# The last mode's product with weights stationary and spectrum moving, straight into Y^T, in a one-core spectral kernel on Trainium2

## The chip, the cores and the metric

The kernel runs on one core of one Trainium2 chip. The metric is device time in microseconds (us) of one execution. The kernel before took 433.02 us, the median of three runs (432.55 to 433.25).

## The reference, cut to what matters

A linear attention (8 batches, 8 heads, 576 rows, head size 64) gives x of 8 x 576 x 512. Then comes a spectral mix: a real Fourier transform over the 576 rows, and for each of the 64 lowest modes a complex product with that mode's own 512 x 512 weights.

```python
Yr = np.einsum('bmd,mde->bme', Xr, w_r) - np.einsum('bmd,mde->bme', Xi, w_i)
Yi = np.einsum('bmd,mde->bme', Xr, w_i) + np.einsum('bmd,mde->bme', Xi, w_r)
...
y = np.fft.irfft(Y, n=S, axis=1)
u = x + y
return (u + np.maximum(u @ w_ch, 0.0)).astype(np.float32)
```

The weights are 2 x 64 matrices of 1 MB in float32. They are each used once, for 8 batches. So the kernel is a stream of weights with little arithmetic per byte. The output stage needs all modes, because the inverse transform sums over them.

## The kernel before

Each mode's product has the spectrum as the stationary operand (32 columns of `xt_c`, of which 16 are wanted: real and imaginary parts of 8 batches) and the weights moving. The four 128-row chunks `dc` of the contraction run side by side in four column strips of the array: in the trace of before, the first four of the last eight products start within 10 ns of each other, at 394.05 us, where whole-array products of the same width (zl) start 109 to 120 ns apart. Their partial sums lie in four groups of 32 partitions. A second set of small "pick" products adds the groups and transposes the result.

```python
def mode_product(kk, ps, stage, yt_ps):
    wr, wi = w_get(kk)
    st = stage.tile([128, D], F16, tag="ystage", bufs=2, name=f"ys{kk}")
    n_part = 2 if kk == NM - 1 else 1          # the last mode: two halves of the columns
    pw = D // n_part
    P = [ps.tile([128, D], F32, tag="P", bufs=2, ...)[:, 0:pw] for i in range(n_part)]
    for t, w in ((1, wr), (0, wi)):
        for i in range(n_part):
            for dc in range(NDC):
                mm = nc.tensor.matmul(
                    P[i][dc * 32 : dc * 32 + 32, :], xt_cols(dc, t, kk),
                    w[:, dc, i * pw : i * pw + pw],
                    start=(t == 1), stop=(t == 0), tile_position=(0, dc * 32))
        if t == 1 and kk >= NM - 4:
            keep_warm(6)                       # products nobody needs, for PE's clock
    if NM - 4 <= kk < NM - 1:
        keep_warm(3)
    for i in range(n_part):                    # casts, VectorE or ScalarE
        dst = st[:, i * pw : i * pw + pw]
        if (kk + i) % 2 == 0: nc.vector.tensor_copy(out=dst, in_=P[i])
        else:                 nc.scalar.copy(out=dst, in_=P[i])
    for ec in range(NDC):                      # sum of four groups, transposed
        mm = nc.tensor.matmul(yt_ps[:, ec, kk % 8, :], st[:, ec * 128 : ec * 128 + 128], pick_sb)
    ...
```

A copy then moves `yt_ps` into `YT` (Y^T: columns of the model on partitions). After the last mode the output stage begins. It forms `zl` from the last eight modes of `YT` and the channel weights, stages it in `last`, and adds the inverse transform into accumulators (`acc`), which are rectified, added and stored.

```python
def keep_warm(n):
    for _ in range(n):
        pin(nc.tensor.matmul(last_ps[0], id16, wch16[:, 0, :]))
...
for h in range(2):                             # zl: first product of the output stage
    for ec in range(NDC):
        nc.tensor.matmul(last_ps[h][:, 0:hw], rows[ec], wch16[:, ec, cols], ...)
```

Weights are loaded by GpSimd-issued DMAs that cast to bfloat16, eight buffers deep, one DMA for each matrix.

Of the kernel before, what the change touches and what calls it, by code (L numbers as in the profile page):

```python
# [10 lines left out]
F32 = mybir.dt.float32  # L11
# [36 lines left out]
def kernel(  # L48
# [10 lines left out]
    nc = tc.nc  # L59

    B, H, S, Dh = q.shape
    D = H * Dh
    NM = moe_w_r.shape[0]
    NHP = H // 2
    NDC = D // 128
    NJJ = 4
    XDC = 3 * B * NM
    XTW = NDC * XDC + 2 * B * NM
    NL = 8
# [23 lines left out]
    xt_c = xpool.tile([128, XTW], BF16, name="xt_c")  # L93
# [3 lines left out]
    def xt_cols(dc: int, t: int, kk: int):  # L97

        c0 = dc * XDC + t * B * NM + kk
        return xt_c[:, c0 : c0 + 31 * NM + 1 : NM]  # L100
# [9 lines left out]
    def w_load(kk: int, half: int, pool, tag: str, bufs: int):  # L110
        name, src = (("wr", moe_w_r), ("wi", moe_w_i))[half]
        w = pool.tile([128, NDC, D], BF16, tag=tag, bufs=bufs, name=f"{name}{kk}")
        tc.keep_in_program_order(
            nc.gpsimd.dma_start(out=w, in_=src[kk].rearrange("(p dc) e -> p dc e", dc=NDC))  # L114
        )
        return w

    w_in: dict[int, list] = {}
# [9 lines left out]
    pin = tc.keep_in_program_order  # L128
# [5 lines left out]
    def w_next():  # L134
        kk, half = pending.pop(0)
        pool, tag, bufs = (wpool, "w", W_KEEP) if kk < n_keep else (wpre, "wp", W_PRE)
        w_in.setdefault(kk, []).append(w_load(kk, half, pool, tag, bufs))
# [187 lines left out]
    def w_get(kk: int):  # L325
        if kk not in w_in:
            w_in[kk] = [w_load(kk, half, wpool, "w", W_KEEP) for half in range(2)]
        return w_in.pop(kk)

    def keep_warm(n: int):  # L330

        for _ in range(n):
            pin(nc.tensor.matmul(last_ps[0], id16, wch16[:, 0, :]))

    def mode_product(kk: int, ps, stage, yt_ps):

        wr, wi = w_get(kk)
        st = stage.tile([128, D], F16, tag="ystage", bufs=2, name=f"ys{kk}")

        n_part = 2 if kk == NM - 1 else 1  # L340
        pw = D // n_part
        P = [
            ps.tile([128, D], F32, tag="P", bufs=2, name=f"P{kk}_{i}")[:, 0:pw] for i in range(n_part)
# [7 lines that stand above are left out]
                        start=(t == 1), stop=(t == 0), tile_position=(0, dc * 32),  # L351
                    )
                    if kk >= NM - 4:
                        pin(mm)
            if t == 1 and kk >= NM - 4:
                keep_warm(6)
# [4 lines that stand above are left out]
            if (kk + i) % 2 == 0:  # L361
                nc.vector.tensor_copy(out=dst, in_=P[i])  # L362
            else:
                nc.scalar.copy(out=dst, in_=P[i])  # L364
        for ec in range(NDC):
            mm = nc.tensor.matmul(  # L366
                yt_ps[:, ec, kk % 8, :], st[:, ec * 128 : ec * 128 + 128], pick_sb
            )
            if kk >= NM - 4:
                pin(mm)  # L370
        if NM - 4 <= kk < NM - 1:
            keep_warm(3)

    while pending:
        w_next()
    tc.keep_in_program_order(
# [6 lines left out]
    psW = tc.alloc_tile_pool(name="psW", bufs=1, space=PSUM, side="left")  # L383
# [9 lines left out]
    YT = ystage.tile([128, NDC, NM, 2 * B], F16, name="YT")  # L393
    yt_ps = None

    def mode(kk: int):
        nonlocal yt_ps
        if kk % 8 == 0:
            yt_ps = psW.tile([128, NDC, 8, 2 * B], F32, tag="yt", bufs=1, name=f"yt{kk // 8}")
        mode_product(kk, psW, ystage, yt_ps)  # L400
        if kk == NM - 2:
            nc.vector.tensor_copy(out=YT[:, :, NE : NM - 1, :], in_=yt_ps[:, :, 0 : NL - 1, :])
        elif kk == NM - 1:
            nc.vector.tensor_copy(out=YT[:, :, NM - 1, :], in_=yt_ps[:, :, NL - 1, :])  # L404
        elif kk % 8 == 7:
            nc.vector.tensor_copy(out=YT[:, :, kk - 7 : kk + 1, :], in_=yt_ps)

    for kk in range(n_early):
        mode(kk)
# [192 lines left out]
    for kk in range(n_early, NM):  # L602
        mode(kk)
        want = min(len(tiles), (kk - n_early + 1) * len(tiles) // n_spread)
        while done < want:
            channel_product(tiles[done])
            done += 1
        if kk >= NE - 1:
            while rows_done < min(B, 2 * (kk - NE + 2)):
                form_rows(rows_done)  # L610
                rows_done += 1
        if kk == NM - 5:
            psB.release()
            acc_pools.append(
                tc.alloc_tile_pool(name="psT0", bufs=1, space=PSUM, side="right", reuse_waits="tile")
            )
            for n in range(N_PRE):
                channels(n)
                for i, t in enumerate(pairs[n]):
                    add_inverse(n, i, t, 1, EARLY)  # L620
            last_ps.append(psW.tile([128, D], F32, tag="zl", bufs=1, name="zl0"))
# [6 lines left out]
    for h in range(2):  # L628
        cols = slice(h * hw, h * hw + hw)
        for ec in range(NDC):  # L630
# [3 lines left out]
                    start=(ec == 0), stop=(ec == NDC - 1),  # L634
# [62 lines left out]
```

## Time and profile before

| What | Value | View |
|---|---|---|
| Time | 433.02 us median | timed runs |
| Last weights landed | 394.01 us after the span's start | chain |
| First zl product | 395.65 us | timeline |
| Last PE work | about 422 us | chain |
| End of the span | 430.9 us | page |

In the views PE is TensorE's matmuls, PEld its weight loads, DVE VectorE, ACT ScalarE, POOL GpSimd and SP SyncE; L348 is line 348 of the kernel. The span is the time from the first instruction to the last. The page's second part cuts it into 40 slices. A digit is the busy share in tenths; PEclk is the granted TensorE clock, in tenths of full speed.

```profile
PE   0357867787018777677776767667787678997992
...
PEclk9996676666559766657658577566555866999997
DMA  8999999999999999999999999999999999993797
GB/s 148 207 208 209 209 209 209 211 213 215 222 211 213 216 212 213 213 213 213 213 214 214 213 213 213 214 214 214 214 214 213 213 213 213 214 213 77 292 330 281
```

DMA is saturated from the second slice to the 36th, at almost one rate. No engine is over the whole of that stretch. The stream of weights sets when the output stage can start. In slices 37 to 39 PE is at 7, 9 and 9 tenths, at full clock.

The chain that ended last, that is the last instruction followed back through what released each step (start, length, what), shows the joint between the two stages:

```profile
377.26 16.75 DMA wi<-in_moe_w_i_dram
...
394.05 0.39 PE P L348 x4
...
394.52 0.38 ACT ys L364
...
394.95 0.40 PE yt L366 x4
...
395.37 0.23 DVE YT L404
...
395.65 1.06 PE zl L632 x8
```

The timeline of the same stretch (start, length, engine, line, operation, output<-inputs, shapes, and in brackets the idle time before it and what ended it):

```profile
394.05 0.48 PE L348 MATMUL P<-wi,xt_c 128*32 128x256 bf16 x8 [0.54 <-DMA wi<-in_moe_w_i_dram]
...
394.52 0.37 ACT L364 CAST ys<-P 128x256 f16<-128x256 f32 x1 [8.32 <-PE P L348]
394.64 0.42 DVE L362 CAST ys<-P 128x256 f16<-128x256 f32 x1 [3.27 <-PE P L348]
...
394.95 0.39 PE L366 MATMUL yt<-pick_sb,ys 128*128 128x16 f16 x4 [0.42 <-ACT ys L364]
395.37 0.22 DVE L404 CAST YT<-yt 128x64 f16<-128x64 f32 x1 [0.30 <-PE yt L366]
```

Four engine steps follow each other after the landing, each waiting for the one before: products, casts, pick products, copy. From landing to zl they take 395.65 - 394.01 = 1.64 us. This text calls that the tail.

### The profile page before, as it was taken

How to read it: one execution, taken by the hardware profiler on the slowest of the kernel's cores; microseconds unless marked ns; L12 is line 12 of the kernel's file. 1: busy time of each engine (PE TensorE's matmuls, PEld its weight loads, DVE VectorE, ACT ScalarE, POOL GpSimd, SP SyncE). 2: the span in 40 equal slices, each digit the busy share in tenths (PEclk: the TensorE clock that was granted, in tenths of full speed). 3: DMA queues.
4: the chain of work that ended last, by engine and by line, in shares of the span. 5: the costliest groups of instructions: out<-in, count | busy, mean ns of one | idle time of the engine just before them, and what ended most of it. 6: DMA issues, size and time to landing. Idle time of an engine off the chain costs nothing. (4 is left out here: it accounts for less than half of the span.)

```text
span 430.9 us, 6215 instructions
## 1 busy us (share of the span) xinstructions
PE 297.7 (69%) x2542; PEld 154.3 (36%) x2542; DVE 176.9 (41%) x334; ACT 147.3 (34%) x228; POOL 92.3 (21%) x166
## 2 busy tenths in 40 slices
PE   0357867787018777677776767667787678997992
PEld 0346656564004233222322223222233226833440
DVE  0699998854004242322322222322223212202793
ACT  3587666631003222222223213222222221302781
POOL 4233232112102222211222112222212221200100
PEclk9996676666559766657658577566555866999997
DMA  8999999999999999999999999999999999993797
GB/s 148 207 208 209 209 209 209 211 213 215 222 211 213 216 212 213 213 213 213 213 214 214 213 213 213 214 214 214 214 214 213 213 213 213 214 213 77 292 330 281
DMA packets 35563, 92.38 MB, mean 214 GB/s; under 512 B 3152, under 2 KB 16336, under 8 KB 35536
## 3 DMA queue, kind: packets, MB, share of 16 engines
q0 software_dynamic: 32016, 82.52, 98.4%
q1 hardware_dynamic: 3520, 9.47, 5.9%
q8 instruction: 20, 0.33, 0.3%
q14 instruction: 7, 0.06, 0.0%
HBM read 164.07 MB, written 9.44 MB: 403 GB/s over the span
## 5 line engine op out<-in xcount | busy, mean ns | idle before, releaser
L468 PE MATMUL eps<-wch,xTw 128*128 128x512 f16 x144 | 61.4, 575 | 3.7 <-DVE xTw L465 3.2
L476 ACT CAST E<-eps 128x512 f16<-128x512 f32 (+1 forms) x40 | 21.3, 544 | 118.8 <-PE eps L468 118.8
L348 PE MATMUL P<-wr,xt_c 128*32 128x512 bf16 (+1 forms) x260 | 45.6, 560 | 23.5 <-DMA wr<-in_moe_w_r_dram 21.5
L348 PE MATMUL P<-wi,xt_c 128*32 128x512 bf16 (+1 forms) x260 | 44.7, 538 | 23.0 <-DMA wi<-in_moe_w_i_dram 23.0
L114 POOL DMA_DIRECT2D wi<-in_moe_w_i_dram x64 | 34.1, 532 | 122.1 <-PE P L348 86.3
L114 POOL DMA_DIRECT2D wr<-in_moe_w_r_dram x64 | 34.1, 532 | 119.0 <-PE P L348 96.8
L453 DVE TENSOR_TENSOR x_main<-nw,rd 128x256 f32<-128x256 f32 x64 | 24.1, 419 | 72.4 <-PE nw L146 72.4
L362 DVE CAST ys<-P 128x512 f16<-128x512 f32 (+1 forms) x33 | 22.5, 681 | 61.6 <-PE P L348 61.5
L348 PEld LDWEIGHTS <-xt_c 128*32 128x32 bf16 x520 | 24.8, 164 | 58.8 <-issue 28.3
L364 ACT CAST ys<-P 128x512 f16<-128x512 f32 (+1 forms) x32 | 18.5, 580 | 72.2 <-PE P L348 72.0
L146 PEld LDWEIGHTS <-qT 64*128 64x128 f16 (+1 forms) x640 | 20.6, 124 | 54.2 <-issue 38.7
L366 PE MATMUL yt<-pick_sb,ys 128*128 128x16 f16 x256 | 17.2, 176 | 32.1 <-DMA pick_sb<-row_pick 21.0
L465 DVE COPY xTw<-xTp 128x512 f16<-128x512 f16 x36 | 15.2, 423 | 46.0 <-PE xTp L463 46.0
L366 PEld LDWEIGHTS <-ys 128*128 128x128 f16 x256 | 13.2, 105 | 53.0 <-issue 24.8
L146 PE MATMUL num<-kv,qT 64*128 64x65 f16 (+1 forms) x320 | 12.9, 217 | 22.0 <-ACT kv L242 17.9
L468 PEld LDWEIGHTS <-xTw 128*128 128x128 f16 x144 | 14.6, 123 | 37.7 <-issue 23.6
L182 ACT ACTIVATE qe<-q 128x1152 f16<-128x1152 f16 x16 | 17.7, 1155 | 22.9 <-DMA q<-in_q_dram 22.9
L211 PE MATMUL qTp<-id,qe 128*128 128x128 f16 x144 | 16.7, 312 | 12.7 <-DVE qe L195 12.3
L460 ACT CAST x16w<-x_main 128x512 f16<-128x512 f32 x32 | 19.8, 619 | 13.0 <-DVE x_main L453 12.4
L265 DVE TENSOR_TENSOR x<-num,rd 128x512 f16<-128x512 f32 x32 | 22.1, 691 | 1.1
L463 PE MATMUL xTp<-id,x16w 128*128 128x128 f16 x144 | 19.5, 278 | 4.0 <-ACT x16w L460 4.0
L562 ACT ACTIVATE acc<-acc 128x512 f32<-128x512 f32 x36 | 19.1, 581 | 5.4 <-PE acc L510 3.8
(65 smaller groups left out, 382.8 us busy)
## 6 DMA issues: line engine op xcount, KB each, us to landing
wr<-in_moe_w_r_dram POOLq DMA_DIRECT2D x64, 512.0 KB, 18.2
wi<-in_moe_w_i_dram POOLq DMA_DIRECT2D x64, 512.0 KB, 18.4
out_dram<-x_main SPq DMA_DIRECT2D x14, 512.0 KB, 4.9
q<-in_q_dram POOLq DMA_DIRECT2D x8, 576.0 KB, 13.3
k<-in_k_dram POOLq DMA_DIRECT2D x8, 576.0 KB, 14.1
v<-in_v_dram POOLq DMA_DIRECT2D x8, 576.0 KB, 16.2
out_dram<-x_main SPq DMA_DIRECT2D x4, 256.0 KB, 4.0
wch<-in_moe_w_ch_dram POOLq DMA_DIRECT2D x1, 512.0 KB, 20.4
```

The source lines that it names most:

```text
L114: nc.gpsimd.dma_start(out=w, in_=src[kk].rearrange("(p dc) e -> p dc e", dc=NDC))
L146: mm = nc.tensor.matmul(num[hpo][orow, c0 : c0 + 65], qT[rows, hpp, h2, cols], kv_sb[rows, hpp, h2, :])
L265: nc.vector.tensor_tensor(out=dst.rearrange("p (o c d) -> p o c d", o=2, c=4), in0=nv[:, :, :, 0:64], in1=rden.unsqueeze(3).broadcast_to([ ...
L348: mm = nc.tensor.matmul(P[i][dc * 32 : dc * 32 + 32, :], xt_cols(dc, t, kk), w[:, dc, i * pw : i * pw + pw], start=(t == 1), stop=(t == 0) ...
L362: nc.vector.tensor_copy(out=dst, in_=P[i])
L366: mm = nc.tensor.matmul(yt_ps[:, ec, kk % 8, :], st[:, ec * 128 : ec * 128 + 128], pick_sb)
L453: nc.vector.tensor_tensor(out=x[orow, o * 256 : o * 256 + 256].rearrange("p (c d) -> p c d", c=4), in0=nv[o][:, :, 0:64], in1=rd_all[b][or ...
L460: nc.scalar.copy(out=x16, in_=x)
L463: nc.tensor.transpose(xT_ps[:, c, :], x16[:, c * 128 : c * 128 + 128], id16)
L468: nc.tensor.matmul(e_ps, xT[:, c, :], wch16[:, c, :], start=(c == 0), stop=(c == NDC - 1))
L476: nc.scalar.copy(out=dst, in_=e_ps[:, cols])
L562: on_bank(n, {i}, nc.scalar.activation(out=a, in_=a, func=AF.Relu))
```

## The change

The intent is a shorter tail. For the last mode alone, the weights become the stationary operand and 16 spectrum columns the moving one. The product then comes out already summed over the chunks and already transposed, so the casts and the pick products vanish. The last imaginary weights land in two pieces, three quarters and one quarter, so that only a quarter of their products is left for after the last landing. The core of the diff:

```diff
-        tc.keep_in_program_order(
-            nc.gpsimd.dma_start(out=w, in_=src[kk].rearrange("(p dc) e -> p dc e", dc=NDC))
-        )
+        rows_of = src[kk].rearrange("(p dc) e -> p dc e", dc=NDC)
+        for dcs in (slice(0, 3), slice(3, 4)) if (kk, half) == (NM - 1, 1) else (slice(0, NDC),):
+            tc.keep_in_program_order(nc.gpsimd.dma_start(out=w[:, dcs], in_=rows_of[:, dcs, :]))
...
+    def last_mode(ps):
+        kk = NM - 1
+        wr, wi = w_get(kk)
+        y_last = ps.tile([128, NDC, 2 * B], F32, tag="P", bufs=2, name="y_last")
+
+        def product(t, w, dcs):
+            for dc in dcs:
+                c0 = dc * XDC + t * B * NM + kk
+                x = xt_c[:, c0 : c0 + (2 * B - 1) * NM + 1 : NM]
+                for ec in range(NDC):
+                    pin(nc.tensor.matmul(
+                        y_last[:, ec, :], w[:, dc, ec * 128 : ec * 128 + 128], x,
+                        start=(t == 1 and dc == 0 and ec == 0), stop=(t == 0 and dc == NDC - 1),
+                        skip_group_check=True))
+
+        product(1, wr, range(NDC))
+        keep_warm(3)
+        product(0, wi, range(3))
+        product(0, wi, range(3, NDC))
+        nc.vector.tensor_copy(out=YT[:, :, kk, :], in_=y_last)
```

Between the real and the imaginary product the old code made six keep-warm products. The new one makes three.

More of the change, by code (lines that the diff above doesn't have):

```diff
@@ L338, in mode_product @@
         st = stage.tile([128, D], F16, tag="ystage", bufs=2, name=f"ys{kk}")
-        n_part = 2 if kk == NM - 1 else 1
+        n_part = 1
         pw = D // n_part
@@ L372, in mode_product @@
             keep_warm(3)
+    def last_mode(ps):
[7 more added lines that the diff above has]
+                for ec in range(NDC):
+                    pin(
+                        nc.tensor.matmul(
+                            y_last[:, ec, :], w[:, dc, ec * 128 : ec * 128 + 128], x,
+                            start=(t == 1 and dc == 0 and ec == 0), stop=(t == 0 and dc == NDC - 1),
+                            skip_group_check=True,
+                        )
+                    )
+        product(1, wr, range(NDC))
[3 more added lines that the diff above has]
+        nc.vector.tensor_copy(out=YT[:, :, kk, :], in_=y_last)
     while pending:
@@ L399, in mode @@
             yt_ps = psW.tile([128, NDC, 8, 2 * B], F32, tag="yt", bufs=1, name=f"yt{kk // 8}")
+        if kk == NM - 1:
+            last_mode(psW)
+            return
         mode_product(kk, psW, ystage, yt_ps)
@@ L402, in mode @@
             nc.vector.tensor_copy(out=YT[:, :, NE : NM - 1, :], in_=yt_ps[:, :, 0 : NL - 1, :])
-        elif kk == NM - 1:
-            nc.vector.tensor_copy(out=YT[:, :, NM - 1, :], in_=yt_ps[:, :, NL - 1, :])
         elif kk % 8 == 7:
```

## The prediction

> **What bounds the kernel now.** The kernel streams weights: in the page's forty slices the DMA share is 0.9 or more from the second slice to about 392 us, at 207 to 214 GB/s, while PE averages 69%, DVE 41%, ACT 34%. In the chain that ended last the stream ends with the last imaginary weights (wi), landed at 394.01 us. From there everything is serial, and PE carries the chain to 421.7 us. So the change touches only the tail between "last weights landed" and "first product of the output stage"; a microsecond taken there is a microsecond of the total.
>
> **The tail before** (chain and timeline): wi landed 394.01; eight P products 394.05; ACT cast of the first half 394.52 (0.37), DVE cast of the second 394.64 (0.42); four "pick" products into yt 394.95, the last two after DVE, done 395.35; DVE copy into YT 395.37 (0.22); first zl product 395.65. Landing to zl: 1.64 us.
>
> **What the change does.** For the last mode it removes both casts, the pick products and 16 half-width P products. It adds 32 products of 128x128 weights by 16 columns straight into Y^T, one POOL issue (0.53 us, 14 us ahead of need), and 128 descriptors. Three keep-warm products go; 16 real-weight products take their place. Otherwise the instruction order of all engines is the same.
>
> After the second wi piece lands only four products and the YT copy remain:
> - Four products of this size (the pick products) took 0.26 us from first start to last end, 170 ns each, so they start about 30 ns apart. [...] Here the moving operand is strided by 128 bytes[...]: loading 32 strided columns of xt_c takes 133 to 170 ns, 128 contiguous ones 97. I allow 0.05 us.
> - Weights can't be loaded before they land; the pick products show load and product starting 10 ns apart, so nearly free.
> - YT copy 0.22 us, with 0.07 us of hand-over.
>
> Landing to zl: 0.04 + 0.31 + 0.02 + 0.22 + 0.05, about 0.65 us. Saved: 1.0 us.
>
> **Does the landing move?** Piece one should land about 0.6 us (a quarter of the 2.42 us between the last two landings) before the second. Its twelve products need about 0.5 us, so they are just done. The early q, k, v loads, with packets of a quarter the size, run at 209 against 213 GB/s, so small descriptors cost little: I estimate 0.05 us, landing 394.06.
>
> **Predicted.** Net saving 0.95 us, all critical; the output stage shifts whole: 433.02 - 0.95 = 432.1 us, 8 in 10 within 431.5 to 432.7 (runs of before spread 0.7). Faster by over 2%: 0.01; within 2%: 0.98; slower: 0.01.
>
> **Right or wrong, in the profile:** the second piece lands at 394.0 to 394.2, 0.5 to 0.7 after the first; the four last products start within 0.1 of it and end within 0.35; the YT copy is 0.22; zl starts 394.6 to 394.8; from zl to the end is unchanged (35.3 us); granted clock stays 1.00 between 377 and 397.
>
> **What would make it wrong:** the second piece costs a fixed time of its own (landing 0.3 us later eats a third of the gain); strided moving columns run far slower, so the twelve products queue behind the landing; fewer keep-warm products let the clock drop; the store stage is limited by DMA and gives the microsecond back.

0.04 + 0.31 + 0.02 + 0.22 + 0.05 = 0.64, "about 0.65". The 0.05 us allowed for the strided operand, which is part of the 0.31, is the author's estimate from the loads that the trace of before shows (133 to 170 ns against 97).

## The result, and the profile after

In the first measurement the changed kernel took 432.51 us in the median of four runs (431.76, 432.79, 433.58, 432.23), against 433.00 for before. The ratio is 0.9992, with a 95% interval of 0.9968 to 1.0015. Ratios here are from the fast runs of one kernel and of before in the same rounds; they can differ by 0.03% from what the medians or means quoted give. The record marks an execution as slow when it lies over 1.5% above the fastest of its kernel.

The profiled run is the 431.76 one, span 429.8 us. Its chain and timeline answer the lines above (`zl<-wch,id` is keep-warm, `zl<-wch,YT` the real product):

```profile
377.61 16.23 DMA wi<-in_moe_w_i_dram
394.49 1.06 PE zl L658 x8
```

```profile
391.39 0.65 PE L386 MATMUL y_last<-xt_c,wr 128*128 128x16 bf16 x16 [0.28 <-DMA wr<-in_moe_w_r_dram]
...
391.87 0.81 PE L333 MATMUL zl<-wch,id 128*128 128x512 f16 x3
...
393.23 0.94 PE L386 MATMUL y_last<-xt_c,wi 128*128 128x16 bf16 x16 [0.55 <-DMA wi<-in_moe_w_i_dram]
393.88 0.17 PEld L386 LDWEIGHTS <-wi 128*128 128x128 bf16 x4 [0.24 <-DMA wi<-in_moe_w_i_dram]
394.21 0.22 DVE L397 CAST YT<-y_last 128x64 f16<-128x64 f32 x1 [3.10 <-PE y_last L386]
```

The last piece landed at 393.84. Four weight loads and products follow, then the copy at 394.21, then zl at 394.49. The tail is 0.65 us, where 1.64 stood. From zl to the end 35.31 us pass, 35.25 before. In this execution all of the gain arrives: 430.9 - 429.8 = 1.1 us.

And yet the four timed runs average only 0.08% under before, and they spread over 1.8 us where before spreads over 0.7. The question is where the microsecond goes in the other executions.

### The profile page after: what moved, and what is told of

The parts are those of the page before. It is cut to its first block, busy times and chain, and to the rows that moved or that the text cites. A ratio compares the mean times of both kernels' runs of the same rounds, so it can differ in the third digit from the quotient of the medians.

```text
span 429.8 us, 6233 instructions
## 1 busy us (share of the span) xinstructions
PE 296.5 (69%) x2551; PEld 153.8 (36%) x2551; DVE 176.5 (41%) x333; ACT 146.8 (34%) x227; POOL 92.8 (22%) x167
## 3 DMA queue, kind: packets, MB, share of 16 engines
q0 software_dynamic: 32160, 82.52, 98.7%
## 4 chain that ended last, share of the span: by engine, by line
DMA 67%; PE 13%; issue 10%; DVE 4%; ACT 2%; POOL 2%; DVEq 0%; POOLq 0%; ACTq 0%
DMA wr<-in_moe_w_r_dram 31%; DMA wi<-in_moe_w_i_dram 25%; DMA k<-in_k_dram 11%; PE acc L536 3%; PE z L517 2%; PE P L348 2%; PE acc L577 2%; DVE x L265 1%; PE eps L494 1%; PE yp L521 1%; ACT ke L182 1%; POOL wi L115 1%; POOL wr L115 1%; DVE k L189 0%; ACT qT L218 0%
## 5 line engine op out<-in xcount | busy, mean ns | idle before, releaser
L348 PE MATMUL P<-wi,xt_c 128*32 128x512 bf16 x252 | 44.7, 553 | 25.9 <-DMA wi<-in_moe_w_i_dram 25.8
L348 PE MATMUL P<-wr,xt_c 128*32 128x512 bf16 x252 | 45.6, 573 | 22.2 <-DMA wr<-in_moe_w_r_dram 20.2
L362 DVE CAST ys<-P 128x512 f16<-128x512 f32 x32 | 22.0, 688 | 60.9 <-PE P L348 60.7
L364 ACT CAST ys<-P 128x512 f16<-128x512 f32 x31 | 18.1, 585 | 65.6 <-PE P L348 65.3
L146 PE MATMUL num<-kv,qT 64*128 64x65 f16 (+1 forms) x320 | 13.8, 228 | 20.6 <-ACT kv L242 18.4
L489 PE MATMUL xTp<-id,x16w 128*128 128x128 f16 x144 | 18.2, 264 | 4.6 <-ACT x16w L486 4.6
```

Source lines behind the costliest of these rows:

```text
L146: mm = nc.tensor.matmul(num[hpo][orow, c0 : c0 + 65], qT[rows, hpp, h2, cols], kv_sb[rows, hpp, h2, :])
L348: mm = nc.tensor.matmul(P[i][dc * 32 : dc * 32 + 32, :], xt_cols(dc, t, kk), w[:, dc, i * pw : i * pw + pw], start=(t == 1), stop=(t == 0) ...
```

## The experiments

Twelve runs were made. Each run's kernel left a trace of its first execution. The other executions have no trace here, only a time, a span and the mean clock over the whole span. That mean can't show one halved window: it would move by about 0.004 (an estimate, 0.5 x 3.4 / 430), and the changed kernel's values run from 0.696 to 0.740, low and high times mixed. So what a trace of these twelve runs shows is always a first execution.

Three theories, in the order in which they arose:

1. The tail is worth its 1.0 us. Rival 1: the small second piece costs a later landing. Rival 2: the store stage gives the gain back.
2. The scatter comes from the landing itself, because single DMA engines lag.
3. The scatter comes from PE's clock: the shorter last mode does so little PE work around the landing that in some executions the clock drops just as the output stage begins.

### Noise, and the parts of the change

The kernel before, as if it were a change. No edit.

> The kernel before, run again as if it were a change. Theory (the tail is 1.0 us shorter after the change and the scatter of a microsecond between runs comes from when the weight stream lands): ratio 1.000 with an interval of about +-0.1%, and in the profile a tail of 1.64 us from the last landing to the first zl product, with the landing itself anywhere within 0.5 us of 394.0. Rival (the runs of one kernel are equal to 0.1 us and the spread of the changed kernel, 431.8 to 433.6, is its own): the five runs of this kernel stay within 0.4 us.

Measured: 432.99 to 433.82 in five runs, ratio 1.0008 (0.9996 to 1.002). The same kernel thus differs from itself by 0.08% between two sets of runs, about 0.35 us in the means. The spread, 0.8 us, lies between what the two sides had named. In the trace the tail is 1.65 us and the landing at 393.86.

The changed kernel again. No edit.

> The changed kernel again, in five rounds. Theory: 0.9 to 1.1 us faster than before in the mean (ratio 0.9975 to 0.9980), tail 0.65 us in the profile. Rival 1 (the second piece delays the landing in a typical run, and the profiled run of the first measurement was merely the luckiest of four): ratio 0.999 or more, the last landing 394.5 or later. Rival 2 (the store stage gives it back): landing and tail as in the first profile, but more than 35.6 us from the first zl product to the end.

Measured: 431.65, 433.21, 433.62, 433.46, 433.68 and 435.10 us, ratio 1.0008 (0.999 to 1.0027). Theory 1 alone fails here: on average there was no gain. But the traced run, the first one, shows the landing at 393.74, the tail at 0.65 and 35.51 us from zl to the end. So this execution shows neither rival. It is 431.65 us, and the others are 1.5 us and more above it.

One piece instead of two:

> The changed kernel with the last imaginary weights in one piece again; only the transposed product is left of the change. Theory: sixteen products instead of four after the last landing, at 31 ns each 0.37 us more, so tail 1.0 us and time 0.3 to 0.4 us above the changed kernel, about 0.6 us under before. Rival 1 (the small second piece costs): landing earlier by as much as the piece costs, so the time is equal to or below that of the changed kernel.

```diff
-        for dcs in (slice(0, 3), slice(3, 4)) if (kk, half) == (NM - 1, 1) else (slice(0, NDC),):
+        for dcs in (slice(0, NDC),):
```

Measured: 432.72 to 434.45, ratio 1.0021 (1.0008 to 1.0034). In the trace the landing is at 394.02 and the tail 1.02 us, as expected: splitting is worth 0.37 us of tail. The mean is 0.3 us above the changed kernel's of the same rounds. The level is too high for theory 1, as for the changed kernel itself.

The split alone, on the kernel before:

> The kernel before with only the last imaginary weights in two pieces; the product is the old one, and five of its eight matmuls still wait for the second piece. Theory: the same time as before within 0.2 us; the second piece lands 0.6 us after the first and no later than the single load did; tail 1.5 to 1.65 us. Rival 1: slower than before by what the piece costs, 0.3 us or more, seen as a later landing.

```diff
-            nc.gpsimd.dma_start(out=w, in_=src[kk].rearrange("(p dc) e -> p dc e", dc=NDC))
+        for dcs in (slice(0, 3), slice(3, 4)) if (kk, half) == (NM - 1, 1) else (slice(0, NDC),):
+            tc.keep_in_program_order(nc.gpsimd.dma_start(out=w[:, dcs], in_=rows_of[:, dcs, :]))
```

Measured: 432.96 to 434.34, ratio 1.0011 (0.9999 to 1.0023), much like the repeat of before in the same rounds (1.0008). The traced run landed late, at 394.99, but not by the piece: the real weights before it, which are not split, had landed late too, at 392.54 against 391.59. The distance from that landing to the last one prices the split. Over ten traces with two pieces it is 2.45 to 2.59 us, mean 2.49; over four with one piece 2.41 to 2.45, mean 2.42. So the second piece costs 0.07 us in these traces, and rival 1 falls.

### The clock

The trace of before holds 40 records of the granted clock. It is 0.50 or 1.00 in each, and every step between them lies on one grid of 3.413 us. A window is one step of that grid.

More keep-warm products:

> The changed kernel with six keep-warm products after the real-weight products, as before the change had, and one after the last product; none of them should delay anything. Theory 3 (new: PE does too little real work around the landing, a 16-column product being a short one, so that in some executions the granted clock drops in the output stage, depending on where the clock's 3.4 us windows fall; the three profiles so far happened not to catch it): the untraced runs come down to 432.1 +-0.3 and their spread shrinks to under 1 us, as those of before. Theory 2 (the scatter is the landing of the weight stream, which differs with how far single DMA engines lag): no change, a mean of 433.3 and a spread over 1.5 us.

```diff
-        keep_warm(3)
+        keep_warm(6)
         product(0, wi, range(3))
         product(0, wi, range(3, NDC))
+        keep_warm(1)
```

Measured: 432.13, 432.44, 432.86, 432.42, 432.15. Ratio 0.9984 (0.9971 to 0.9997), a gain of 0.8 us in the mean, and a spread of 0.7 us where the changed kernel had 3.5 in its repeat. (The two were measured in different rounds, and k1's interval meets those of the changed kernel's two measurements: on the mean alone, seven against three is not clear of noise.) The tail in the trace is 0.65 us as before, so the seven products delay nothing.

No keep-warm products in the last mode:

> The changed kernel with no keep-warm product in the last mode. Theory 3: slower and wider than the changed kernel, mean above 433.6, and if the profile catches it the granted clock is under 1.00 somewhere between 394 and 402 us and the stretch from the first late product to PE's end is over 25.2 us. Theory 2: the same as the changed kernel, clock 1.00, 25.15 us.

```diff
         product(1, wr, range(NDC))
-        keep_warm(3)
         product(0, wi, range(3))
```

Measured: 432.67 to 435.65, mean 434.20, ratio 1.0024 (1.0005 to 1.0043): the slowest kernel. This run and k1 shared their rounds and their intervals don't overlap, so between none and seven keep-warm products the time does change. Its profile caught a drop of the clock. The windows (stretch, length, busy time and count of PE, PEld, DVE, ACT, POOL, granted clock, DMA share, GB/s):

```profile
391.20:394.70 3.50, 1.63 (x34) 1.15 (x34) 0.36 (x2) 0.00 (x0) 0.00 (x0) 0.99 0.26 48
394.70:398.10 3.40, 3.22 (x15) 1.93 (x16) 0.42 (x1) 1.27 (x3) 0.21 (x1) 0.50 0.00 0
398.10:401.50 3.40, 3.40 (x18) 1.48 (x17) 1.45 (x3) 1.74 (x4) 2.69 (x6) 1.00 0.32 100
```

The clock is halved for exactly one window of 3.4 us, which starts with zl. Up to the first late product (`acc<-last`) 2.49 us pass from zl, instead of 1.66, and PE's stage from there takes 25.58 us instead of 25.15. Together that is 1.3 us.

Removing products cannot prove what the changed kernel itself does. So two more looks at it, without an edit:

> One more look at the changed kernel, for its clock around the landing. Theory 3: either the clock holds and the time is near 431.8 us, or it is 0.50 for one window of 3.4 us within 392 to 402 us, PE's stage is 0.4 to 1.7 us longer, and the time is over 432.8 us. The windows decide: those profiled so far ended at 393.9 and 392.0 and held.

> The same as the run before it, for a second draw of the clock's phase: clock held and about 431.8 us, or one window at 0.50 and over 432.8 us.

The first took 433.73 us, the second 431.62. The first has the drop:

```profile
389.60:393.00 3.40, 2.87 (x29) 1.10 (x27) 1.26 (x2) 0.00 (x0) 0.00 (x0) 1.00 0.67 125
393.00:396.40 3.40, 2.24 (x29) 1.72 (x30) 0.65 (x2) 0.88 (x2) 0.00 (x0) 1.00 0.02 3
396.40:399.80 3.40, 3.40 (x9) 1.21 (x8) 0.00 (x0) 2.13 (x5) 2.90 (x6) 0.50 0.21 62
399.80:403.20 3.40, 3.21 (x15) 1.26 (x14) 2.51 (x3) 1.34 (x3) 0.00 (x0) 1.00 0.49 170
```

In the second the windows fell differently, and the clock held:

```profile
390.20:393.60 3.40, 2.58 (x38) 1.23 (x34) 0.62 (x1) 0.00 (x0) 0.00 (x0) 1.00 0.48 90
393.60:397.00 3.40, 2.58 (x21) 1.69 (x22) 0.65 (x2) 1.57 (x4) 0.50 (x1) 1.00 0.00 0
397.00:400.40 3.40, 3.40 (x17) 1.46 (x15) 1.97 (x3) 1.93 (x4) 2.40 (x6) 1.00 0.45 146
```

The groups of the late products show the price of one of them. The first line is the look with the drop, the second the look without (line, engine, operation, output<-inputs, shapes, count, busy us, mean ns, idle before), both between 396.2 and 399.8 us:

```profile
L536 PE MATMUL acc<-last,inv_sb 128*128 128x512 f16 x5 | 2.4, 606 | 0.4 <-DVE last L666 0.4
```

```profile
L536 PE MATMUL acc<-last,inv_sb 128*128 128x512 f16 x8 | 2.5, 378 | 0.4 <-DVE last L666 0.4
```

PE's stage, from the first late product to PE's end, is 26.82 us with the drop and 25.14 without. That 1.68 us is more than the tail saves. All else is equal to 0.3 us: landing 393.94 and 393.67, tail 0.65 and 0.65.

The run with seven keep-warm products had its windows at the same place as the look with the drop, 392.9 to 396.3, and held:

```profile
392.90:396.30 3.40, 2.69 (x32) 1.75 (x31) 0.65 (x2) 0.89 (x2) 0.00 (x0) 1.00 0.06 11
396.30:399.70 3.40, 3.40 (x17) 1.56 (x16) 1.29 (x2) 2.12 (x5) 2.89 (x6) 1.00 0.22 62
```

So with the same phase, in one execution each, three keep-warm products failed and seven sufficed. That the drop occurs in the changed kernel, and that it costs more than the tail saves when it does, is shown by a2. That it is what takes the gain away in the mean is inferred. For it speak k1 and k2, and the changed kernel's twelve runs: four at 431.6 to 432.2, eight at 432.8 to 435.1, and of the four with a trace the three low ones held the clock and the high one did not. Against it speak three things. The kernels with three keep-warm products left seven traces (after, a1, a2, a3, w1, t1, p1), and only one has the drop, while eight of the twelve times are high; first executions may not be typical. The highest time, 435.10, lies 3.5 us above the lowest, more than one such drop costs. And t1 against b1, below, shows no gain from the added products.

In the trace of after, too, every step of the clock lies on a grid of 3.4 us and its values are 0.50 and 1.00; the halved windows of a2 and k2 above are one step long. The grid's phase differs between executions: in the changed kernel's traces the last window before 394 us starts at 393.90, 392.07, 392.96 and 393.64. No wait as long as a window came before the drops: in a2 PE's longest wait in the window that preceded the drop was 0.54 us (in k2 1.16 us), and 16 of its 29 products there had 16 columns. What amount of work keeps the clock stays open. Neither the profile's busy time nor the sum of moving columns in a window sorts the traces. In a2, PE was busy for 2.24 us of the window before the drop; in before the clock held after a window with the same 2.24 us (394.00 to 397.41), and in n1 after one with 2.13 us (392.50 to 395.90). The look that fell and the repeat a1 that held both had 3,328 columns in their window, by a count in the trace.

### The landing

The other part of the scatter is theory 2. The page counts 16 DMA engines, and the trace has sixteen semaphore records for each load of weights, which are read here as one for each engine. The load is complete with the last of them: for the last load of before that record is at 394.01 us, and the first product that reads it starts at 394.05. The records give the sixteen landings in order of time, though not which engine each belongs to. For the last load of before, in us after the fastest engine (390.12):

```
0.0 0.3 0.4 0.5 0.8 0.9 0.9 | 2.5 2.5 2.6 2.8 2.8 | 3.4 3.8 3.8 3.9
```

These distances stay nearly the same from load to load until one of the sixteen falls back, by about 0.9 us or a little more, and it does not catch up. In before, the last of the sixteen lands 2.83 us after the first for the load that begins to land at 242.7 us, 3.71 for the next one, and 3.89 for the last load; a packet of the instruction queue starts at 246.5. The falls coincide with such packets, the instruction fetches. In that trace the sum of the sixteen distances, compared between loads four apart, rises by 0.9 to 1.5 us over each of the nine fetches from 175 to 372 us. Elsewhere from 165 us on it moves by 0.3 us or less, but for a rise of up to 0.9 us near 285 us, where no fetch is. The DMA part of the page counts the fetches:

```profile
q8 instruction: 20, 0.33, 0.3%
```

Each is one packet of 16,384 bytes. Eighteen of them come before 375 us and take 893 to 975 ns. Their lengths repeat with a period of eight (893, 893, 948, 945, 935, 974, 975, 961), as if eight engines took them in turn. Two rounds of eight put eight engines back twice, and two more put two of them back a third time. The groups above, though blurred by different starts, look like that; it is inferred, since no record names the engine. In this stream a fetch is not free, by the rise of the sum above. That it keeps a DMA engine from the weights is inferred from the times; the next expectation states it as seen.

How many fetches the next two edits take away or add can be estimated from the trace of before: 4,577 records of PE products and weight loads start before 375 us, with 18 fetches, so about 254 for each. By that, 640 fewer are 2.5 fetches less, and 2400 more are 9.4 fetches more.

Fewer PE instructions, with the same work. The numerator products took two half-height products per head pair. With K^T V stored block-diagonally, one product does both; results stay correct:

> The changed kernel with the same work in 640 fewer PE instructions (the attention products of two head halves joined over a block-diagonal K^T V; results stay right). In the six traces so far, the 16 KB instruction fetches (about 0.93 us each, 18 of them before 375 us) each put one DMA engine behind for good, and the engines end in groups about one microsecond apart, as if eight engines had taken two fetches each and two of these a third; the last landing is that of an engine with three. Theory 2: with 15 or 16 fetches before 385 us no engine has a third one, the spread of the last landing over the engines falls from 3.3 to 3.9 us to about 2.5 to 2.9, and the last landing comes about 0.9 us earlier, near 393.0; time 0.9 us under the changed kernel. Theory 3: the landing may move but the spread of the times stays over 1.5 us.

```diff
-                for hpo in range(2):
-                    rows = slice(hpo * 64, hpo * 64 + 64)
-                    c0 = (hpp * 2 + h2) * 65
-                    mm = nc.tensor.matmul(
-                        num[hpo][orow, c0 : c0 + 65], qT[rows, hpp, h2, cols], kv_sb[rows, hpp, h2, :]
-                    )
+                o4 = num[hpp][orow, 0:260].rearrange("p (o t n) -> p o t n", o=2, t=2)
+                mm = nc.tensor.matmul(o4[:, :, h2, :], qT[:, hpp, h2, cols], kv_sb[:, hpp, h2, :, :])
... (and, earlier in the kernel)
-    kv_all = [xpool.tile([128, 2, 2, 65], F16, tag="kv", bufs=B, name=f"kv{b}") for b in range(B)]
+    kv_all = [xpool.tile([128, 2, 2, 2, 65], F16, tag="kv", bufs=B, name=f"kv{b}") for b in range(B)]
```

(The cut parts reorder the heads to match, set the tiles to zero once, and place two small constants in the unused end of `xt_c` to make room.) The page's line for it:

```profile
q8 instruction: 17, 0.28, 0.2%
```

Measured: 431.39, 432.41, 430.56, 430.68, 430.41, 432.10; ratio 0.9956 (0.994 to 0.9972). Fifteen fetches come before 375 us, a sixteenth at 379.7. The spread over the engines is 3.04 us and the landing 393.38: earlier than the changed kernel's mean of 393.80 over four traces, but by 0.42 us and not by 0.9. The mean of the times, 431.26 us, is 1.8 us under the changed kernel's 433.04, twice the forecast and far more than the traced landing explains; the rest stays open. (The edit also changes the attention stage, but the stream as a whole isn't earlier: its fastest engine lands at 390.34, the changed kernel's at 390.28 to 390.40.) The spread is 2.0 us, over 1.5 as theory 3 had it. Whether the clock makes that spread isn't shown: the one trace held it, at 431.39, and the three runs a microsecond under that one have no trace.

More PE instructions:

> The changed kernel with 24 tiny unneeded products (32 columns of weights, one moving column) before each of the modes 10 to 59, 2400 PE instructions more, which should need nine or ten more instruction fetches of 16 KB. Theory 2: 27 fetches before 375 us, that is a fourth on some engines: spread of the last landing 4.2 to 4.9 us, landing 394.6 to 395.0, time 0.9 us above the changed kernel. Rival (the fetches have nothing to do with the lag): spread and landing as in the changed kernel. If PE itself becomes the limit in the stream, landing will be later by much more and the run says nothing.

```diff
+    N_PAD = 24
...
+        if n_early <= kk < NM - 4:
+            for _ in range(N_PAD):
+                nc.tensor.matmul(P[0][0:32, 0:1], id16[:, 0:32], id16[:, 0:1])
```

```profile
q8 instruction: 29, 0.48, 0.4%
```

Measured: 433.14 to 435.04, ratio 1.0017 (1.0003 to 1.0031). There are 27 fetches before 375 us, nine more than in before; the spread over the engines is 4.60 us and the landing 395.10, which is 1.3 us after the changed kernel's mean of 393.80. The fastest engine lands at 390.50, as in all the traces (390.1 to 390.5). So the stream itself didn't slow down; only the landings behind fell further behind. The mean is 0.4 us over that of the changed kernel's repeat, measured in other rounds, and less than the 0.9 expected and than the landing says; why is not shown.

The fewer instructions on the kernel before, and both remedies together:

> The kernel before with the same 640 fewer PE instructions and nothing else of the change. It keeps its six keep-warm products and its long products, so theory 3 costs it nothing. If the change is worth its tail once the clock holds, it is 0.9 to 1.0 us slower than the run with both remedies: about 431.4 us; tail 1.64 us in the profile. If it is equal to that run, the transposed product gains nothing.

> Both remedies: the changed kernel with 640 fewer PE instructions and seven keep-warm products in the last mode. If the two causes add: 430.5 us in the mean, 2.6 us under before (ratio 0.994), spread of the runs under 1.2 us; clock 1.00 to the end of PE's work, 25.15 us from the first late product to PE's end, tail 0.65 us, spread of the last landing over the engines 2.5 to 3.1 us.

```diff
+                o4 = num[hpp][orow, 0:260].rearrange("p (o t n) -> p o t n", o=2, t=2)
+                mm = nc.tensor.matmul(o4[:, :, h2, :], qT[:, hpp, h2, cols], kv_sb[:, hpp, h2, :, :])
...
-        keep_warm(3)
+        keep_warm(6)
         product(0, wi, range(3))
         product(0, wi, range(3, NDC))
+        keep_warm(1)
```

The first part, the edit of t1, is in both, in b2 on the kernel before and in b1 on the changed kernel. The second part, the edit of k1, is in b1 alone.

Measured in the same rounds: b2 431.91 to 432.48, ratio 0.9975 (0.9962 to 0.9987); b1 431.02 to 432.12, ratio 0.9961 (0.9948 to 0.9975). Fewer instructions alone take 1.1 us off before. The landing in b2's trace is 392.96, its spread 2.59. In b1's trace the landing is 393.59, its spread 3.41: one engine lagged 0.7 us behind the next for a reason that the trace doesn't show. The count of fetches thus goes with the direction and part of the size of the landing, over three counts: with 15 fetches before 375 us the spread is 2.59 to 3.41 us (b2, t1, b1), with 18 it is 3.89 in before and 3.48 in after, with 27 it is 4.60 (p1). It does not explain every engine's lag.

Between b1 and b2 lies what the change is worth with seven keep-warm products: 0.14% in the ratios, whose intervals overlap, and 0.65 us in the means (431.46 against 432.11). That is less than the 0.9 to 1.0 expected. In the traces the tails differ by 0.99 (0.65 against 1.64), and the landings by 0.63 the other way. b1 beats both kernels: its mean is 431.46 us, against 433.23 for before in the same rounds and 433.04 over the changed kernel's twelve runs.

But b1 misses its own expectation by 1.0 us (430.5 in the mean): the two remedies don't add. And it doesn't beat t1, which lacks only the four added keep-warm products: 0.9956 (0.994 to 0.9972) for t1, 0.9961 (0.9948 to 0.9975) for b1, in different rounds. Only the spread is smaller, 1.1 us against 2.0. With three keep-warm products and fewer instructions, the changed kernel is thus at least as fast as with seven. Theory 3 as the account of the mean doesn't fit this pair, and no run here resolves it; both kernels in the same rounds, with a trace of every execution, would.

The readings, one trace each, all read as in the chain and timeline above:

| Run | Last landing | Tail | First late product to PE's end | zl to end of span | us |
|---|---|---|---|---|---|
| before | 394.01 | 1.64 | 25.14 | 35.25 | 432.72 |
| n1, before again | 393.86 | 1.65 | 25.15 | 35.68 | 432.99 |
| s1, split only | 394.99 | 1.55 | 25.15 | 35.96 | 434.34 |
| after | 393.84 | 0.65 | 25.15 | 35.31 | 431.76 |
| a1, after again | 393.74 | 0.65 | 25.14 | 35.51 | 431.65 |
| a2, after, look | 393.94 | 0.65 | 26.82 | 37.21 | 433.73 |
| a3, after, look | 393.67 | 0.65 | 25.14 | 35.48 | 431.62 |
| w1, one piece | 394.02 | 1.02 | 25.15 | 35.66 | 432.72 |
| k1, 7 keep-warm | 393.82 | 0.65 | 25.15 | 35.73 | 432.13 |
| k2, 0 keep-warm | 394.01 | 0.66 | 25.58 | 36.73 | 433.36 |
| t1, fewer PE instructions | 393.38 | 0.65 | 25.15 | 35.57 | 431.39 |
| p1, more PE instructions | 395.10 | 0.66 | 25.15 | 35.64 | 433.17 |
| b1, both remedies | 393.59 | 0.65 | 25.13 | 35.16 | 431.15 |
| b2, before, fewer PE instructions | 392.96 | 1.64 | 25.13 | 35.60 | 432.04 |

Landing plus tail plus the last column but one is the span. With the clock held, PE's stage is constant to 0.02 us. The time between zl and the end varies by 0.8 us among these, in the last stores, with no order by kernel. Rival 2 therefore falls.

## Why the prediction was right or wrong

- **Where the kernel is bound: right.** The stream and then a serial joint; the traces add up.
- **The tail: right to the hundredth.** Predicted 0.65 us from 1.64; measured 0.65 in every trace of the product with two pieces, but for 0.66 twice. The copy is 0.22. The four last products take 0.29 us, predicted 0.31.
- **The strided moving operand: right.** One product takes 192 ns where the pick products took 170. Sixteen take 0.65 us, so they start (0.65 - 0.19) / 15 = 31 ns apart, as the contiguous ones did.
- **The second piece: right.** 0.05 us predicted, 0.07 measured; it lands 0.65 us after the first (the foreseen 0.6). The page counts 144 packets more in the weights' queue (32,160 against 32,016), 16 of them under 512 B; the other 128 are the number foreseen.
- **The output stage shifts whole: right as far as the stores go**, wrong as far as PE goes.
- **The clock: wrong.** The step that failed reads "Three keep-warm products go; 16 real-weight products take their place", and with it "granted clock stays 1.00 between 377 and 397". Sixteen products of 16 columns are short: they end 0.65 us after they begin, and 0.55 us of waiting follow the three keep-warm products that are left. In a2 the clock fell to 0.50 for one window and PE's stage grew by 1.68 us. The prediction named this among its risks and gave it no weight in the sum. The mean of twelve runs is 433.04 us: no gain over before (432.95 to 433.23 in its rounds), where 0.95 us was predicted. That the drop accounts for this in the mean is inferred: with seven keep-warm products (k1) the gain is 0.8 us, and 0.65 between b1 and b2, but t1 gains without them.
- **The scatter: wrong.** The range rested on the 0.7 us by which the three runs of before spread. The changed kernel's scatter is larger, 3.5 us over twelve runs. The first measurement's median, 432.51, lies inside the range of 431.5 to 432.7; the repeat's, 433.54, does not, and only four of the twelve executions do. That the first median fell inside was luck of the draw; the tail under it was foreseen rightly.

## What to carry to other kernels

A filler product for the clock can be part of the critical path's price list (none of them against seven, k2 against k1, was 434.20 against 432.40 us in the mean): when real work in a joint gets shorter, count what is left of PE's work in each clock window (3.41 us here), look at the clock of more than one execution, and try filler where PE only waits. One profile of such a kernel is one draw, so compare spreads as well as medians. Test a remedy alone and on top of the others: here two that each helped did not add. In this DMA-limited kernel instructions were traffic too: with 640 fewer of them the page counts 17 fetches of 16 KB instead of 20, and the time was 1.1 us under before (b2).
